# Scale factors of the head on GpSimd and ScalarE, zeroing inside the list, and mode switches known to the planner: a linear-attention and max-of-three feed-forward kernel

## The chip, the cores and the metric

The kernel runs on one core of a Trainium2 chip. The metric is the device time of one execution in microseconds (us). Engines are named as in the profile: PE is TensorE (PEld its weight loads), DVE is VectorE, ACT is ScalarE, POOL is GpSimd, SP is SyncE, whose queue issues most of the DMAs.

## The reference

Inputs r, k, v have the shape (4, 8, 768, 48) for batch, heads, sequence and head dimension; w and u are (8, 48). Each head keeps a 48x48 state:

```python
for t in range(S):
    kt, vt, rt = (k[:, :, t], v[:, :, t], r[:, :, t])
    cur = np.einsum('bhd,bhe->bhde', u[None] * kt, vt)
    y[:, :, t] = np.einsum('bhd,bhde->bhe', rt, state + cur)
    state = w[None, :, :, None] * state + np.einsum('bhd,bhe->bhde', kt, vt)
```

The result y, as 3072 tokens of 384 numbers, goes through a feed-forward layer with three up matrices (384x768) and one down matrix (768x384): `h = max(max(x @ w1, x @ w2), x @ w3)`, out = `h @ w_out`, all in float32.

## The kernel before

The recurrence is worked off in 12 chunks of 64 positions. A chunk has two parts q of 8 units each (a unit is a batch and a pair of heads on 2 x 64 partitions). In a chunk the decay w**t is multiplied into k and r (`scale`, L466), so that the state is only needed at the chunk's edges: `scores` are the products of keys and queries, `mask` keeps those of earlier positions, the diagonal holds r·(u k), `values` makes the output from masked scores and state, `keys` the addition to the state. Chunks 0 and 1 (`WHOLE`) do this in float32 on 64x64 quarters of PE (`whole`, L531), and take the diagonal from a product called the bonus (`bonus`, with `r_u` on ACT before it and `on_diagonal`, L558, on DVE behind it); their keys by position come from a product too (`flipped`, L565). Chunks 2 and 3 (up to `CORNERS`) split each operand into a high and a low float16 part and still use 64x64 quarters (L524). From chunk 4 on the split operands stand in `Block`s, tiles with two 64x64 blocks on the diagonal of a 128x128 square and zeros beside them; `spread` copies dense blocks into them by DMA, and PE uses its full array (L521). Up to chunk 2 DVE does the scalings; behind that GpSimd does (`helper`).

The feed-forward part works on a chunk's 256 tokens at a time: 18 `up` groups of 9 matmuls and 3 `down` groups of 18 (L651). x is also split in two float16 parts, and its last 96 rows are moved by six small DMAs (`x_last`, L635). The weights come as 64-bit words, eight tiles of 1152 KB; each is converted by ACT (`tops`, L340), DVE (`convert`, L344), ACT (`round_up`, L347) and DVE (`leave`, L350). Three buffers hold words (`raw64`); the tile `pw` of decay powers uses one of them at first. `stir` (L647) and `blank` (L640) are matmuls on a zero tile whose results nobody reads; there are 30 stirs of 3 matmuls, in a chain.

Ahead of the list, written by hand: loads of w, u and constants (L287 to L292), the zeroing of two tiles `ztop` and of the 14 blocks on POOL (L331, L415) and of the state (L439), and on DVE the decay powers (scans, L366) with the factors sc, wrt, wc, wcv, uw, dg, wck (L370 to L390).

Everything else is given to `Plan` by `do(due, engine, cost, fn, reads, writes, takes)`. Its `order` is a list scheduler that runs while the kernel is built: with a cost for each entry, a lag per engine, a model of the DMAs and of PE's clock, and start times for the engines (`free`), it picks the entry that can start first, and among those of one engine that can start within 0.02 us the one with the smallest due number. `SHIFT` adds a number per kind of entry and stage (five columns: due below 0, from 0, from 1, from 2, from 10) to the due number. The entries are then written out in order of their planned starts, and each engine takes its queue in that order; at run time an engine waits for semaphores, not for planned times.

Of the kernel before, what the change touches and what calls it, by code (L numbers as in the profile page):

```python
# [18 lines left out]
P = 128  # L19
# [52 lines left out]
class Plan:  # L72
# [4 lines left out]
    BEFORE, BEHIND, PHASE, LANES = 1.5, 1.0, 1.4, 8  # L77
    CLASSES = (0.0, 1.0, 2.0, 10.0)
    SHIFT = {
        "sp feat": (3.37, -2.28, 2.83, -0.27, 0),  # L80
        "sp tok": (-0.37, -1.28, 2.64, 0.03, 0),
        "dve tkf": (0, 0.35, 0, 0, 0),
        "pe turned": (0, -0.88, 0, 0, 0),
        "act tkt": (0, -2.47, 0, 0, 0),
        "dve kT": (-0.62, -26.75, 0, 0, 0),
        "dve rT": (1.01, -35.26, -13.5, 0, 0),
        "act ru": (1.08, 1.39, 0, 0, 0),
        "pe bo": (-1.74, -0.21, 0, 0, 0),
        "dve am": (0, -0.03, 0.19, 2.29, 8.79),
        "pe sc": (6.74, 6.37, 4.36, -0.11, 0.12),  # L90
        "pe va": (-1.39, -2.73, -1.75, -0.08, 0),
        "act xh": (1.82, -0.83, 0.07, -0.97, -3.12),
        "dve xl": (0.58, 0, -2.36, -1.28, 1.02),
        "sp x3": (-1.49, -1.21, 0.13, -4.67, -1.28),
        "act xsq": (0, 0.01, 0, 2.16, -1.69),
        "pe stir": (0, -4.85, -11.53, -2.89, 0),
        "sp word": (2.21, 2.24, 0, 0, 0),
        "act ztop": (4.76, 27.48, 0, 0, 0),
        "dve word": (0, -2.64, 0, 0, 0),
        "act his": (3.42, 1.73, 0, 0, 0),  # L100
# [144 lines left out]
def kernel(ctx, tc, feat, tok, wu, ut, ws, wo, cst, out):  # L245
# [594 lines left out]
    def act(columns):  # L843
        return 0.11 + 0.83e-3 * columns
# [304 lines left out]
```

## Time and profile before

| | us |
|---|---|
| median of three runs | 393.11 |
| the three runs | 390.78, 393.11, 394.2 |
| the profiled execution | 390.22 |
| its span, first to last instruction | 388.2 |
| PE busy / DVE busy / ACT busy / POOL busy | 375.1 / 243.0 / 244.3 / 185.2 |
| mean granted clock of PE | 0.993 |

The span is what the trace covers; 2.0 us of the execution lie around it. Busy shares are means over stages: in the head (to about 80 us) the recurrence's first chunks, the weights' conversion and the first feed-forward chunks overlap; the middle repeats chunk by chunk; the last 40 us are feed-forward alone.

### The profile page before, as it was taken

What the parts mean: (1) busy time and instruction counts of PE and PEld (TensorE: products, weight loads), DVE (VectorE), ACT (ScalarE), POOL (GpSimd) and SP (SyncE); (2) the same over time, 40 slices, a digit from 0 to 9 for tenths busy, and PEclk for the clock granted to TensorE, in tenths of its full rate; (3) what the DMA queues carried; (4) which work ended last, traced back from release to release, by engine and by line L of the source; (5) the groups of instructions that cost most, each with busy time, mean ns of one, the idle gap of its engine ahead of it and who ended that gap; (6) DMA issues with size and microseconds to landing.
All of it is one profiled execution on the core that took longest, in us unless ns stands there. A gap on an engine that the chain in (4) does not pass through costs nothing.

```text
span 388.2 us, 13560 instructions
## 1 busy us (share of the span) xinstructions
PE 375.1 (97%) x5652; PEld 337.8 (87%) x5652; DVE 243.0 (63%) x464; ACT 244.3 (63%) x618; POOL 185.2 (48%) x187
## 2 busy tenths in 40 slices
PE   6998999899999999999999999999999999999993
PEld 4877988788889999999999999999999999998883
DVE  7397999868568597558557557456467466232350
ACT  3478986587547566566566566566556865696621
POOL 9600032359975683673673683674673550020110
PEclk8999999999999999999999999999999999999999
DMA  8866673324852994994994996994994994903201
GB/s 273 342 206 248 207 281 116 138 82 143 231 186 88 298 251 125 288 299 134 276 300 156 279 234 163 300 284 128 305 256 114 279 253 104 293 24 144 77 2 49
DMA packets 27989, 77.23 MB, mean 199 GB/s; under 512 B 4881, under 2 KB 12561, under 8 KB 26897
## 3 DMA queue, kind: packets, MB, share of 16 engines
q1 hardware_dynamic: 27776, 76.19, 66.1%
q8 instruction: 46, 0.75, 0.9%
q14 instruction: 23, 0.18, 0.2%
q10 hardware_dynamic: 144, 0.10, 0.1%
HBM read 38.38 MB, written 4.72 MB: 111 GB/s over the span
## 4 chain that ended last, share of the span: by engine, by line
PE 91%; POOL 4%; DVE 1%; ACT 1%; issue 1%; DVEq 0%; POOLq 0%
PE psm L651 72%; PE psv L521 8%; PE psa L521 3%; PE psv L524 2%; PE psv L531 2%; PE psm L647 1%; PE psa L531 1%; PE psa L524 1%; PE psa L565 1%; POOL ztop L331 1%; ACT am L497 1%; POOL ktd L415 0%; POOL vd L415 0%; POOL kd L415 0%; POOL sb L415 0%
## 5 line engine op out<-in xcount | busy, mean ns | idle before, releaser
L651 PEld LDWEIGHTS <-w 128*128 128x128 f16 x2592 | 250.2, 98 | 29.6 <-issue 0.7
L651 PE MATMUL psm<-x,w 128*128 128x256 f16 x1944 | 219.7, 273 | 0.0
L679 POOL TENSOR_TENSOR hl<-m,hh 128x256 f16<-128x256 f32 x60 | 44.6, 745 | 130.2 <-ACT hh L673 125.1
L670 DVE SCALAR_TENSOR_TENSOR m<-psm,m 128x256 f32<-128x256 f32 x144 | 60.2, 419 | 60.6 <-PE psm L651 52.5
L673 ACT CAST hh<-m 128x256 f16<-128x256 f32 x72 | 29.0, 402 | 56.2 <-DVE m L670 55.8
L651 PE MATMUL psm<-hh,w 128*128 128x256 f16 x432 | 56.3, 273 | 0.5 <-issue 0.5
L466 POOL TENSOR_TENSOR feat<-feat,wrt 128x512 f32<-128x512 f32 x36 | 49.1, 1376 | 7.0 <-DMA feat<-in_feat_dram 7.0
L485 POOL TENSOR_TENSOR am<-tok,u_sb 128x384 f32<-128x384 f32 x18 | 20.8, 1157 | 45.1 <-DVE al L584 45.1
L449 ACT ACTIVATE junk<-tok 128x384 bf16<-128x384 f32 x72 | 37.4, 520 | 3.3 <-DMA tok<-in_tok_dram 2.1
L666 ACT ACTIVATE m<-psm 128x256 f32<-128x256 f32 x72 | 27.2, 378 | 14.0 <-PE psm L651 12.7
L651 PE MATMUL psm<-hl,w 128*128 128x256 f16 x216 | 33.4, 273 | 0.0
L628 DVE SCALAR_TENSOR_TENSOR x<-psv,x 112x512 f16<-112x512 f32 x24 | 16.5, 688 | 22.6 <-ACT x L624 22.1
L624 ACT ACTIVATE x<-psv 112x512 f16<-112x512 f32 x24 | 14.3, 594 | 15.4 <-PE psv L521 14.4
L521 PE MATMUL psv<-rh,sb 128*128 128x64 f16 x256 | 23.6, 193 | 0.0
L521 PE MATMUL psv<-ah,vb 128*128 128x64 f16 x256 | 23.6, 193 | 0.0
L521 PE MATMUL psv<-al,vb 128*128 128x64 f16 x128 | 22.7, 193 | 0.0
L521 PE MATMUL psv<-rl,sb 128*128 128x64 f16 x128 | 22.7, 193 | 0.0
L499 POOL TENSOR_TENSOR am<-cs,a 128x512 f32<-128x512 f32 x18 | 20.0, 1114 | 3.4 <-DVE a L490 3.3
L490 DVE TENSOR_REDUCE a<-am 128x8 f32<-128x384 f32 x20 | 11.0, 549 | 16.9 <-POOL am L486 16.9
L521 PEld LDWEIGHTS <-vb 128*128 128x128 f16 x384 | 21.1, 98 | 0.4
L574 DVE COPY_PREDICATED am<-cs,psa 128x512 f32<-128x512 int32 x24 | 17.7, 736 | 5.6 <-PE psa L521 5.0
L696 ACT ACTIVATE io<-psm 128x256 f32<-128x256 f32 x36 | 13.4, 381 | 11.1 <-PE psm L651 11.0
(119 smaller groups left out, 579.2 us busy)
## 6 DMA issues: line engine op xcount, KB each, us to landing
tok<-in_tok_dram SPq DMA_DIRECT2D x26, 576.0 KB, 6.3
feat<-in_feat_dram SPq DMA_DIRECT2D x24, 512.0 KB, 4.6
raw<-in_ws_dram SPq DMA_DIRECT2D x6, 1152.0 KB, 7.1
out_dram<-io SPq DMA_DIRECT2D x36, 128.0 KB, 4.8
vb<-vd SPq DMA_DIRECT2D x16, 256.0 KB, 6.9
sb<-sd SPq DMA_DIRECT2D x16, 256.0 KB, 6.9
kb<-kd SPq DMA_DIRECT2D x16, 256.0 KB, 6.6
vb<-vd SPq DMA_DIRECT2D x16, 248.0 KB, 6.8
```

Source lines behind the costliest of these rows:

```text
L449: nc.scalar.activation(out=junk[:, 0:U * D].rearrange("p (u d) -> p u d", u=U), in_=src, func=AF.Square, scale=scale, accum_out=stat[:, ki ...
L466: helper(c).tensor_tensor(out=t[n], in0=t[n], in1=tb, op=ALU.mult)
L485: helper(c).tensor_tensor(out=w.rearrange("p (g b) d -> p g b d", g=2), in0=t["r"], in1=by_token(u_sb, q), op=ALU.mult)
L499: helper(c).tensor_tensor(out=t["a"], in0=eye.unsqueeze(1).broadcast_to([P, U, C]), in1=t.pop("sum").unsqueeze(2).broadcast_to([P, U, C]), ...
L521: nc.tensor.matmul(out=ps[:, i, :], lhsT=block[k].on[a][i], rhs=prods[k](b, i), **flags)
L574: nc.vector.copy_predicated(out=t["a"], mask=strict.unsqueeze(1).broadcast_to([P, U, C]), data=t.pop("sc"))
L628: nc.vector.scalar_tensor_tensor(out=x_part(x, 1, q), in0=ps, scalar=sc_x(c), in1=x_part(x, 0, q), op0=ALU.mult, op1=ALU.subtract)
L651: nc.tensor.matmul(out=ps, lhsT=a, rhs=b, start=first and n == 0, stop=last and n == len(prods) - 1)
L666: nc.scalar.mul(out=m, in_=ps, mul=by)
L670: nc.vector.scalar_tensor_tensor(out=m, in0=ps, scalar=by, in1=m, op0=ALU.mult, op1=ALU.max)
L673: nc.scalar.copy(out=h[0][:, f, :], in_=m)
L679: lows_by(c, f).tensor_tensor(out=h[1][:, f, :], in0=m, in1=h[0][:, f, :], op=ALU.subtract)
```

## The change

Loads of w, constants and u are issued from ACT's queue, in this order, so that SP's starts with the features. wc, uw and dg are made on POOL, wcv and wck on ACT; sc stays on DVE as a scalar_tensor_tensor with a tile of ones. The scaling of u enters the list. tkf (decay factors for the token layout, transposed by PE into tkt) takes the buffer of `ru`. Blocks are no longer zeroed whole ahead of the list: entries "pad" zero only the columns that nothing writes, and the spreads read their keys. The state is not zeroed any more (chunk 0 writes it whole). `state1` is made on ACT. An entry says whether it uses quarters (`corner`), and a change between that and the full array costs `TURN` in the plan. Scores wait for the bonus, values of q = 1 for those of q = 0, the ups of a chunk for those of the chunk before (from chunk 2 on). `ah` and `al` get two buffers. `SHIFT` has new numbers in all its rows (a few are shown), and the engines' planned start times are new.

```diff
@@ -74,81 +74,83 @@
...
-    BEFORE, BEHIND, PHASE, LANES = 1.5, 1.0, 1.4, 8
+    BEFORE, BEHIND, PHASE, LANES, TURN = 1.5, 1.0, 1.4, 8, 0.095
...
     SHIFT = {
-        "sp feat": (3.37, -2.28, 2.83, -0.27, 0),
...
-        "dve tkf": (0, 0.35, 0, 0, 0),
...
-        "pe bo": (-1.74, -0.21, 0, 0, 0),
...
-        "pe sc": (6.74, 6.37, 4.36, -0.11, 0.12),
...
-        "pe stir": (0, -4.85, -11.53, -2.89, 0),
...
-        "act ztop": (4.76, 27.48, 0, 0, 0),
...
-        "pe kp": (5.05, -0.04, 0, 0, 0),
...
-        "pe up": (0, 23.33, 26.76, 0, 0.29),
...
+        "sp feat": (-1.56, 4.21, 2.31, 0.8, 0),
...
+        "act u": (0, 2.03, 0, 0, 0),
+        "pool pad": (0, -9.82, -1.24, 0, 0),
+        "dve tkf": (0, -2.54, 0, 0, 0),
...
+        "pe bo": (0.16, 2.71, 0, 0, 0),
...
+        "pe sc": (4.94, 1.67, -0.08, 0.08, 7.28),
...
+        "pe stir": (0, 0, -1.82, 7.69, -19.34),
...
+        "act ztop": (15.57, 7.02, 0, 0, 0),
...
+        "pe kp": (2.37, -0.61, 0, 0, 0),
...
+        "pe up": (0, 0, -0.08, 0.26, -1.61),
...
     }
...
@@ -216,6 +218,9 @@
...
+            if e == "pe" and p["corner"] != corner:
+                corner = p["corner"]
+                cost += self.TURN
@@ -284,12 +289,12 @@
...
     wu_sb = const.tile([P, 2, NP], F32, name="wu_sb")
-    nc.sync.dma_start(out=wu_sb, in_=wu)
+    nc.scalar.dma_start(out=wu_sb, in_=wu)
     w_sb, uf_sb = wu_sb[:, 0], wu_sb[:, 1]
+    cs = const.tile([P, 2 * P + 2], F32, name="cs")
+    nc.scalar.dma_start(out=cs, in_=cst)
     u_sb = const.tile([P, NP, D], F32, name="u_sb")
     nc.scalar.dma_start(out=u_sb, in_=ut)
-    cs = const.tile([P, 2 * P + 2], F32, name="cs")
-    nc.sync.dma_start(out=cs, in_=cst)
@@ -366,64 +371,68 @@
         nc.vector.tensor_tensor_scan(
...
+    one4 = ones[:, 0:NP]
     sc = const.tile([P, NP], F32, name="sc")
     nc.vector.reciprocal(out=sc, in_=pw[:, :, C // 2])
-    nc.vector.tensor_scalar(out=sc, in0=sc, scalar1=SC_R, scalar2=None, op0=ALU.mult)
+    nc.vector.scalar_tensor_tensor(out=sc, in0=sc, scalar=SC_R, in1=one4, op0=ALU.mult, op1=ALU.mult)
     wrt = const.tile([P, NP, C], F32, name="wrt")
     nc.vector.tensor_tensor(out=wrt, in0=pw[:, :, 0:C], in1=sc.unsqueeze(2).broadcast_to([P, NP, C]), op=ALU.mult)
     wkt = wrt[:, :, ::-1]
-    wc = const.tile([P, NP], F32, name="wc")
-    nc.vector.tensor_copy(out=wc, in_=pw[:, :, C])
-    wcv = const.tile([P, NP], F32, name="wcv")
-    nc.vector.tensor_scalar(out=wcv, in0=wc, scalar1=SC_V, scalar2=None, op0=ALU.mult)
-    uw = const.tile([P, NP], F32, name="uw")
-    nc.vector.tensor_tensor(out=uw, in0=uf_sb, in1=w_sb, op=ALU.mult)
+    wc, wcv, wck, uw = (const.tile([P, NP], F32, name=n) for n in ("wc", "wcv", "wck", "uw"))
+    nc.gpsimd.tensor_tensor(out=wc, in0=pw[:, :, C], in1=one4, op=ALU.mult)
+    nc.gpsimd.tensor_tensor(out=uw, in0=uf_sb, in1=w_sb, op=ALU.mult)
     dg = const.tile([P, NP, D], F32, name="dg")
-    nc.vector.tensor_tensor(out=dg, in0=eye[:, 0:D].unsqueeze(1).broadcast_to([P, NP, D]), in1=wc.unsqueeze(2).broadcast_to([P, NP, D]), op=ALU.mult)
-    tkf = const.tile([P, NP, 2, C], F32, name="tkf")
+    nc.gpsimd.tensor_tensor(out=dg, in0=eye[:, 0:D].unsqueeze(1).broadcast_to([P, NP, D]), in1=wc.unsqueeze(2).broadcast_to([P, NP, D]), op=ALU.mult)
+    nc.scalar.mul(out=wcv, in_=wc, mul=SC_V)
+    nc.scalar.mul(out=wck, in_=wc, mul=SC_KT / SC_R)
...
     def both():
+        tkf = work.tile([P, U, C], F32, name="ru").rearrange("p (g h) s -> p g h s", h=2)
+        turned.append(tkf)
         for hh in range(2):
             nc.vector.tensor_tensor(out=tkf[:, :, hh, :], in0=wkt, in1=wck.unsqueeze(2).broadcast_to([P, NP, C]), op=ALU.mult)
...
-    wck = const.tile([P, NP], F32, name="wck")
-    nc.vector.tensor_scalar(out=wck, in0=wc, scalar1=SC_KT / SC_R, scalar2=None, op0=ALU.mult)
     tkt = const.tile([P, NP, D], F32, name="tkt")
-    nc.scalar.mul(out=u_sb, in_=u_sb, mul=SC_A)
...
+    def u_scaled():
+        nc.scalar.mul(out=u_sb, in_=u_sb, mul=SC_A)
...
     turned = []
...
     def turn():
         tps = psa.tile([P, NP, P], F32, name="psa")
         for g in range(NP):
-            nc.tensor.transpose(out=tps[:, g, :], in_=tkf[:, g].rearrange("p a s -> p (a s)"), identity=ident)
+            nc.tensor.transpose(out=tps[:, g, :], in_=turned[0][:, g].rearrange("p a s -> p (a s)"), identity=ident)
         turned.append(tps)
...
     def turned_back():
         for hh in range(2):
             hs = slice(hh * C, (hh + 1) * C)
-            nc.scalar.copy(out=tkt[hs], in_=turned[0][hs, :, hh * C:hh * C + D])
...
+            nc.scalar.copy(out=tkt[hs], in_=turned[1][hs, :, hh * C:hh * C + D])
...
+    W = P if CORNERS < NCH else C
...
     class Block:
...
-        def __init__(self, name, w):
-            n = 2 * U * w
-            t = bd.tile([P, n + P - w], F16, name=name)
-            nc.gpsimd.memset(t.bitcast(F32), 0.0)
-            self.flat, self.w = t[:, 0:n], w
+        def __init__(self, name, used=None):
+            n, w = 2 * U * W, used or 0
+            t = bd.tile([P, n + P - W], F16, name=name)
+            self.flat = t[:, 0:n]
             self.dense = self.flat.rearrange("p (s u n) -> p s u n", s=2, u=U)
-            self.on = [[t[:, (s * U + i) * w:(s * U + i) * w + P] for i in range(U)] for s in range(2)]
+            self.on = [[t[:, (s * U + i) * W:(s * U + i) * W + P] for i in range(U)] for s in range(2)] if W == P else None
+            self.blank = self.dense.bitcast(F32)[:, :, :, w // 2:]
...
-    kd, ktd, vd, sd = ([Block(f"{n}{q}", P) for q in range(2)] for n in ("kd", "ktd", "vd", "sd"))
-    kb, ktb = (Block(n, P) for n in ("kb", "ktb"))
-    vb, sb = ([Block(f"{n}{q}", P) for q in range(2)] for n in ("vb", "sb"))
+    kd, ktd, vd, sd = ([Block(f"{n}{q}", w) for q in range(2)] for n, w in (("kd", C), ("ktd", D), ("vd", D), ("sd", D)))
+    kb, ktb = (Block(n) if W == P else None for n in ("kb", "ktb"))
+    vb, sb = ([Block(f"{n}{q}") if W == P else None for q in range(2)] for n in ("vb", "sb"))
@@ -436,7 +445,6 @@
...
     state = const.tile([P, NP, B, D], F32, name="state")
-    nc.gpsimd.memset(state, 0.0)
@@ -880,7 +888,7 @@
...
     def spreading(c, due, dst, src, keys, name):
         if c >= CORNERS:
-            dma(due, lambda: spread(nc.sync, dst, src), 2.4, reads=keys, writes=[name], n=2)
+            dma(due, lambda: spread(nc.sync, dst, src), 2.4, reads=[*keys, *(("pad", n) for n in range(14))], writes=[name], n=2)
@@ -907,7 +915,7 @@
...
-        do(due - 0.16, h, 2 * cost, lambda: product(c, q), reads=[t], takes=[("am", ("am", c, q))], writes=[("kdec", c, q)], near=0.55)
+        do(due - 0.16, h, 2 * cost, lambda: product(c, q), reads=[t, "u"], takes=[("am", ("am", c, q))], writes=[("kdec", c, q)], near=0.55)
@@ -936,17 +944,17 @@
...
-        do(due - 0.27, "pe", 0.96, lambda: bonus(c, q), reads=[f, ("kT", c, q), ("ru", c, q)], takes=[("psa", ("bo", c, q))], counts=0.5)
+        do(due - 0.27, "pe", 0.88, lambda: bonus(c, q), reads=[f, ("kT", c, q), ("ru", c, q)], writes=[("bonus", c, q)], takes=[("psa", ("bo", c, q))], counts=0.5, corner=True)
...
-        scored(c, q, due, [f, ("kT", c, q), ("rT", c, q)])
+        scored(c, q, due, [f, ("kT", c, q), ("rT", c, q), ("bonus", c, q)])
...
     def whole_values(c, q, due):
         sbs = [("sd", q), ("rT", c, q), ("feat", c, q)] if c else []
-        do(due, "pe", 0.92 * (1 + (c > 0)), lambda: values(c, q), reads=[("am", c, q), ("tok", c, q), *sbs], takes=[("psv", ("va", c, q))], counts=0.5)
+        do(due, "pe", 0.89 * (1 + (c > 0)), lambda: values(c, q), reads=[("am", c, q), ("tok", c, q), *sbs, *[("valued", c)] * q], writes=[("valued", c)] * (not q), takes=[("psv", ("va", c, q))], counts=0.5, corner=True)
...
@@ -963,14 +971,14 @@
...
         if c + 1 < WHOLE:
-            do(due + 0.06, "dve", 0.5, lambda: nc.vector.tensor_scalar(out=state1[q], in0=sf, scalar1=S16, scalar2=None, op0=ALU.mult), reads=[s], writes=[("sd", q)])
+            do(due + 0.06, "act", act(U * D), lambda: nc.scalar.mul(out=state1[q], in_=sf, mul=S16), reads=[s], writes=[("sd", q)])
...
     def valued(c, q, due, reads):
         reads = [*reads, *held(c, [("sdh", q), ("sdl", q)], ("sb", q))]
@@ -1012,7 +1020,8 @@
...
-                do(due + 0.035 * i, "pe", 0.983, mul, reads=[*x, *((a, f, h) for a in ("his", "lo") for h in parts[i])], takes=[("psm", ("up", c, f, i))])
+                do(due + 0.035 * i, "pe", 0.983, mul, reads=[*x, *((a, f, h) for a in ("his", "lo") for h in parts[i]), *[("upped", c - 1)] * (c > 1)],
+                   writes=[("upped", c)] * (f == NF - 1), takes=[("psm", ("up", c, f, i))])
@@ -1051,7 +1060,11 @@
...
-    do(0.1, "dve", 0.7, both, writes=["tkf"])
+    do(0.1, "act", 0.36, u_scaled, writes=["u"])
+    if W == P:
+        for n, b in enumerate([*kd, *ktd, *vd, *sd, kb, ktb, *vb, *sb]):
+            do(0.5 + 0.1 * n, "pool", 1.0 if n > 7 else 0.7, lambda b=b: nc.gpsimd.memset(b.blank, 0.0), writes=[("pad", n)])
+    do(0.1, "dve", 0.7, both, takes=[("ru", "tkf")])
@@ -1080,7 +1093,7 @@
...
-    order = plan.order(dict(pe=1.5, dve=5.2, act=3.0, pool=13.0, sp=1.6))
+    order = plan.order(dict(pe=1.5, dve=4.7, act=4.4, pool=5.4, sp=0.75))
...
```

## Rows read from the trace of the kernel before

**Rows 1.** The page of the profile: span, and PE's busy time, share and instructions.

```profile
span 388.2 us, 13560 instructions
PE 375.1 (97%) x5652; PEld 337.8 (87%) x5652; DVE 243.0 (63%) x464; ACT 244.3 (63%) x618; POOL 185.2 (48%) x187
```

**Rows 2.** Busy time by stretch: stretch and its length, busy us (instructions) of PE, PEld, DVE, ACT and POOL, granted clock of PE, DMA share, GB/s. The last two rows are of DVE alone.

```profile
8.00:9.00 1.00, 1.00 (x7) 0.69 (x6) 1.00 (x3) 0.81 (x3) 1.00 (x2) 0.50 1.04 436
...
40.00:50.00 10.00, 10.00 (x185) 9.02 (x181) 9.90 (x15) 9.11 (x14) 0.91 (x2) 1.00 0.71 247
...
70.00:80.00 10.00, 8.52 (x281) 7.24 (x279) 8.22 (x17) 7.94 (x23) 2.00 (x2) 1.00 0.40 141
...
140.00:170.00 30.00, 30.00 (x420) 27.43 (x419) 22.20 (x39) 17.63 (x48) 17.12 (x18) 1.00 0.84 234
...
0.00:40.00 40.00, 27.56 (x51) 0.96 0.72 259
40.00:70.00 30.00, 29.86 (x44) 1.00 0.55 196
```

**Rows 3.** Groups of PE's instructions by line and shape: count, busy us, mean ns of one, idle before.

```profile
L651 PE MATMUL psm<-x,w 128*128 128x256 f16 x1944 | 219.7, 273 | 0.0
...
L647 PE MATMUL psm<-still 128*128 128x256 f16 x90 | 13.6, 306 | 1.1 <-DVE still L266 1.1
```

**Rows 4.** The chain of waits that ended last, in order of time: start, us, what. The stretch in which it leaves PE.

```profile
63.49 5.03 PE psm L651 x45
...
69.16 1.21 DVE tok L505
...
71.20 2.03 ACT am L497 x8
...
74.47 0.73 PE psv L524 x44
```

**Rows 5.** Timeline of DVE in the head: start us, us, line, operation, out<-in; in brackets the idle time before and what ended it.

```profile
3.65 0.18 DVE L370 RECIPROCAL sc<-raw 128x4 f32<-128x4 f32 x1
3.86 0.74 DVE L371 TENSOR_SCALAR sc<-sc 128x4 f32<-128x4 f32 x1
...
4.64 0.42 DVE L373 TENSOR_TENSOR wrt<-raw,sc 128x256 f32<-128x256 f32 x1
4.98 0.54 DVE L376 COPY wc<-raw 128x4 f32<-128x4 f32 x1
...
6.36 0.08 DVE L443 MEMSET stat<- 128x24 f32 x1
6.48 0.76 DVE L387 TENSOR_TENSOR tkf<-wrt,wck 128x256 f32<-128x256 f32 x2
7.16 2.49 DVE L466 TENSOR_TENSOR feat<-feat,wrt 128x512 f32<-128x512 f32 x4
...
14.10 0.69 DVE L558 TENSOR_TENSOR am<-psa,cs 128x512 f32<-128x512 f32 x1 [4.45 <-PE psa L531]
...
16.68 0.36 DVE L966 TENSOR_SCALAR state<-state 128x384 f32<-128x384 f32 x1 [1.11 <-ACT state L600]
```

**Rows 6.** Timeline of POOL, ACT and PE in the head, in the same form.

```profile
7.30 0.81 PE L398 MATMUL psa<-cs,tkf 128*128 128x128 f32 x4 [2.11 <-DVE tkf L387]
...
8.81 0.91 ACT L548 ACTIVATE ru<-feat,uw 128x256 f32<-128x256 f32 x2
...
12.90 1.15 PE L531 MATMUL psa<-ru,feat 64*64 64x64 f32 x32
...
15.26 0.74 POOL L439 MEMSET state<- 128x768 f32 x1
...
16.03 0.54 ACT L600 COPY state<-psv 128x192 f32<-128x192 f32 x2 [0.97 <-POOL state L439]
...
17.12 1.48 ACT L340 CAST ztop<-raw 128x1152 f16<-128x1152 bf16 x1
...
36.82 2.14 PE L651 MATMUL psm<-x,w 128*128 128x256 f16 x18
```

**Rows 7.** SP's queue: the issue of the first features (timeline), and all loads of features (page: count, KB each, median us from issue to landing).

```profile
1.66 0.43 SPq L272 DMA_DIRECT2D feat<-in_feat_dram  x1
...
feat<-in_feat_dram SPq DMA_DIRECT2D x24, 512.0 KB, 4.6
```

**Rows 8.** Groups by line and shape that are nearest to the moved products: a GpSimd product of 256 columns over the whole run (page), and of the first 47 us ScalarE's groups and GpSimd's smallest memset.

```profile
L679 POOL TENSOR_TENSOR hl<-m,hh 128x256 f16<-128x256 f32 x60 | 44.6, 745 | 130.2 <-ACT hh L673 125.1
...
L429 ACT ACTIVATE sd<-state 128x384 f16<-128x384 f32 x2 | 1.0, 522 | 0.0
...
L449 ACT ACTIVATION_READ_ACCUMULATOR junk<-state 128x1 f32 x4 | 0.8, 192 | 0.0
...
L1136 POOL MEMSET const-float32-1.0<- 128x1 f32 x1 | 0.1, 98 | 0.0
```

**Rows 9.** Timeline of POOL and DVE: a GpSimd product, and the same scaling on DVE beside it and alone.

```profile
53.76 1.44 POOL L679 TENSOR_TENSOR hl<-m,hh 128x256 f16<-128x256 f32 x1 [2.69 <-ACT hh L673]
...
54.92 0.83 DVE L466 TENSOR_TENSOR feat<-feat,wrt 128x512 f32<-128x512 f32 x1
...
56.34 0.68 DVE L466 TENSOR_TENSOR feat<-feat,wrt 128x512 f32<-128x512 f32 x1
```

**Rows 10.** Timeline of PE's weight loads at the change from the full array to quarters, with the idle time before it.

```profile
62.54 0.83 PEld L524 LDWEIGHTS <-kd 64*64 64x64 f16 x48 [0.21 <-issue]
```

More of the change, by code (lines that the diff above doesn't have):

```diff
@@ L146 @@
+        "pe count": (0, 0, 0, 0, -0.24),
+        "dve flag": (0, 0, 0, 0, 0.89),
     }
@@ L149, in __init__, with do @@
         self.bufs, self.todo, self.wrote, self.read = bufs, [], {}, {}
-    def do(self, due, eng, cost, fn, reads=(), writes=(), takes=(), move=0, near=0, parts=1, counts=1.0):
+    def do(self, due, eng, cost, fn, reads=(), writes=(), takes=(), move=0, near=0, parts=1, counts=1.0, corner=False):
         n = len(self.todo)
@@ L168, in do @@
         need.discard(n)
-        self.todo.append(dict(n=n, due=due, eng=eng, cost=cost, fn=fn, need=need, takes=takes, move=move, near=near, parts=parts, counts=counts, kind=kind, stage=stage, base=base, touch={*reads, *writes, *new}))
+        self.todo.append(dict(n=n, due=due, eng=eng, cost=cost, fn=fn, need=need, takes=takes, move=move, near=near, parts=parts, counts=counts, corner=corner, kind=kind, stage=stage, base=base, touch={*reads, *writes, *new}))
     def order(self, free):
@@ L185, in order @@
         ready = [p["n"] for p in self.todo if not p["need"]]
-        out, taken = [], {pool: [] for pool in self.bufs}
+        out, taken, corner = [], {pool: [] for pool in self.bufs}, False
         def earliest(p):
@@ L577, in a_high @@
         t = raws[c, q]
-        t["ah"] = work.tile([P, U, C], F16, name="ah")
+        t["ah"] = work.tile([P, U, C], F16, name="ah", bufs=2)
         nc.scalar.copy(out=t["ah"], in_=t["a"])
@@ L918, in before_keys @@
         if c < WHOLE:
-            do(due - 0.30, "pe", 0.76, lambda: flipped(c, q), reads=[("feat", c, q), ("kT", c, q)], takes=[("psa", ("kp", c, q))], counts=0.5)
+            do(due - 0.30, "pe", 0.70, lambda: flipped(c, q), reads=[("feat", c, q), ("kT", c, q)], takes=[("psa", ("kp", c, q))], counts=0.5, corner=True)
             do(due - 0.30, "act", act(U * D), lambda: flipped_back(c, q), reads=[("kp", c, q)], takes=[("kt", ("kt", c, q))])
@@ L956, in keyed @@
     def keyed(c, q, due, reads):
-        do(due, "pe", 0.76 if c < WHOLE else 0.64 if c < CORNERS else 0.62, lambda: keys(c, q), reads=reads, takes=[("psv", ("ke", c, q))], counts=0.5 if c < WHOLE else 1.0)
+        do(due, "pe", 0.72 if c < WHOLE else 0.64 if c < CORNERS else 0.62, lambda: keys(c, q), reads=reads, takes=[("psv", ("ke", c, q))], counts=0.5 if c < WHOLE else 1.0, corner=c < CORNERS)
         s = ("state", q)
@@ L972, in valued @@
         reads = [*reads, *held(c, [("sdh", q), ("sdl", q)], ("sb", q))]
-        do(due, "pe", 1.43 if c < CORNERS else 1.42, lambda: values(c, q), reads=[*reads, ("ah", c, q), ("al", c, q), ("rh", c, q), ("rl", c, q)], takes=[("psv", ("va", c, q))])
+        do(due, "pe", 1.43 if c < CORNERS else 1.42, lambda: values(c, q), reads=[*reads, ("ah", c, q), ("al", c, q), ("rh", c, q), ("rl", c, q), *[("valued", c)] * q], writes=[("valued", c)] * (not q), takes=[("psv", ("va", c, q))], corner=c < CORNERS)
         leave_x(c, q, due)
```

120 lines of the change are left out of this document (59 added, 61 removed).

## The prediction

> **What bounds the kernel now.** First the page: TensorE (PE) is busy for 375.1 of 388.2 us [rows 1], so the end can only come forward by the time in which PE idles or does work that counts for nothing. Then the stretches [rows 2]: from 140 to 170 us, as in all the middle, PE is busy for the whole 30 us, and nothing in the change takes matmuls from there. The gaps are in the first 80 us. Then PE's groups [rows 3]: 90 matmuls on a zeroed tile ("stir", 13.6 us) fill waits in that head. The first matmul of the feed-forward part starts at 36.82 us [rows 6], and from there PE is nearly full until 68.5 us.
>
> There the chain of waits is the important view [rows 4]: it leaves PE and runs through VectorE's decay of the tokens and ScalarE's eight diagonals before PE can go on at 74.47. VectorE was busy 29.86 of the 30 us before 70, and PE only 8.52 of the 10 us after 70 [rows 2]. So PE has used up what VectorE had prepared. Where VectorE idled is before 40 us: 27.56 us busy of 40 [rows 2]. **A head that is shorter on PE alone would wait again near 70 us; a gain has to be an earlier VectorE.** That is my measure for each part.
>
> **The scale factors.** VectorE's order by hand is: scans, reciprocal 0.18, sc 0.74 (at 3.86), wrt (at 4.64), and from 4.98 the copy wc, then wcv, uw, dg and wck, until the memset of stat at 6.36 and the first listed work, tkf, at 6.48 [rows 5]. The change takes wc to wck away: 6.36 - 4.98 = 1.4 us. The op on sc stays, in another form; from 3.86 to 4.64 it held the queue 0.78 us, while the reciprocal on the same 128x4 tile took 0.18. Between these ends (nothing won, 0.6 won) I take 0.5, as the neighbour is of the same size and on the same engine. Listed work starts 1.9 us earlier, at about 4.6.
>
> Is the rest there by then? tkf needs wck, now scan, GpSimd, ScalarE. No GpSimd product of four columns is shown: from below a 0.10 us memset, from above the 0.745 of 256 columns; for ScalarE 0.19 (one column read out [rows 8]) and 0.27 (half of the two copies of 192 columns at 16.03 [rows 6]). From the scans' end at 3.6, wck is then ready between 4.1 and 5.0 counting both ScalarE products, at the worst 0.4 us behind a start at 4.6 and still 1.4 us ahead of 6.48. dg and uw follow on GpSimd by 5.8 at the worst, ahead of their readers. Feature loads move to the front of SP's queue: the first was issued at 1.66 behind two others [rows 7] and now goes at about 0.75; with the 4.6 us that such a load takes to land [rows 7] that is 5.4, just when a tkf of 0.76 that starts at 4.6 is through. The three small loads now pass one after another through ScalarE's queue, which has nothing else until wcv; u is third and has no early reader. I cost that at nothing; if the cover fails, the factors wait about 0.8 us (two issues of 0.4).
>
> **The zeroing.** GpSimd's list of memsets ended with state at 15.26 to 16.0, and ScalarE's first copy into state waited for it, 0.97 us [rows 6]. Left as it was, this would have kept a chunk 0 that comes 1.9 us earlier from gaining anything behind that copy: the memsets do not depend on VectorE. Its removal is therefore the condition of the first term and has no term of its own. The smaller memsets go behind the factors on GpSimd; their first readers are the spreads of chunk 4, far behind 80 us, and GpSimd has little else so early (0.91 us busy from 40 to 50 [rows 2]). Cost nothing; without that cover, one memset, of about the 0.74 that state took, would stand in front of a product.
>
> **state1 to ScalarE.** Two products of 0.36 [rows 5] leave VectorE and become two of about 0.5 on ScalarE (0.522 for the same columns, [rows 8]). VectorE gains 0.7, but ScalarE was busy 9.11 of the 10 us from 40 to 50 [rows 2] and feeds the weights. Between 0 and 0.7 I take 0.4.
>
> **The order.** VectorE idled from 9.65 to 14.10 for the bonus scores [rows 5]. Their left operand was ready at 9.72 (ScalarE, 8.81 + 0.91), but PE did two other products first and started the bonus at 12.90 [rows 6]: up to 3.2 us too late. Behind PE's idle 2.11 us the clock had fallen to its 1.2 GHz level (granted 0.50 from 8 to 9 [rows 2, 6]). In the new list the scores wait for the bonus by a key, and the flips are due behind it; I take half, 1.6, between 0 (ordered as late as before) and 3.2. That VectorE would use the time is likely: weight 0 could be converted, which waited until 17.12 [rows 6].
>
> **Corners.** Some 15 groups of 64-row products lie among 128-row ones before 122 us; each enters with 0.21 us in which the weight loads stand still [rows 10], of which little shows in PE's own row. If a few of these turns go, it is between 0 and 15 x 0.21 = 3.2; I take 0.3, since the list must still alternate.
>
> **Sum.** 1.9 + 0.4 + 1.6 + 0.3 = 4.2 us. Against the profiled execution, 390.22 (span 388.2 and 2.0 around it), this gives 386.0. That execution was faster than all three runs shown (390.78, 393.11, 394.2); the mean of the four is 392.1, so 1.9 more has to be added for a typical run: **388 us** (387.9).
>
> **The rivals.** *The gain is absorbed* (0 to 3 us; 389.1 to 392.1). VectorE and GpSimd can hold each other up: beside GpSimd's product of 53.76 a scaling took 0.83 us, alone 0.68 [rows 9], and beside memsets the copy of four columns took 0.54 and the tensor_scalar 0.74 [rows 5]. Now three GpSimd products run beside sc, wrt and tkf. If VectorE waits out each, at up to 0.745, that is 2.2 us: 4.2 - 2.2 leaves 2.0, so 390.1. For it speak the rows; against it, that the two small products are over before 5 us. The Trainium skill (SBUF — State Buffer, "Who interferes with whom") says that a VectorE op with two SBUF inputs contends with a GpSimd op that reads SBUF, and not with one that only writes it. By that rule the new neighbours are worse for wrt and tkf than the memsets were; the 0.83 agrees with it. The same band holds the case that the last weights come no earlier because their words land no earlier.
>
> *The whole head moves* (6.5 to 9 us; 383.1 to 385.6): all of the 3.2, all of the switches that lie in the head, and VectorE's idle 4.45 us filled with weight 0. For it: VectorE idles 12.4 us before 40. Against it: the weights' words, which land no faster.
>
> *The stirs stand in the way* (slower). In the new table the stirs from the tenth on have due numbers from -9.3, ahead of most products. Freed early, 20 of them at 3 x 0.113 = 0.34 us (1944 matmuls of the same size in 219.7 us [rows 3]) put 6.8 us between the bonus and the values of chunk 0, and PE takes its queue in order. Against the 2.6 us of the other terms that is 4.2 slower: 396.3. It decides from 2.6 us of stirs that are not in a wait, eight of them. Against it: PE idled up to the transposes at 7.30, and the more stirs go there, the fewer are left.
>
> That the change does not do what it says has no case of its own here: the ops are moved in plain sight; only the order that the list works out is not seen, and this is in the bands.
>
> **How the numbers follow.** Forecast (gain 3 to 6.5, 385.6 to 389.1) 0.47; absorbed 0.30; whole head 0.13; stirs 0.10. A measurement of this kernel tells 1% from no change, that is below 389.2 or above 397.0 against 393.11. Faster: 0.44 of the forecast and 0.13 make 0.57. Slower: half of the stirs' case, 0.05. Same 0.38. The range runs from 383 to 393: it takes in the forecast, the absorbed case with 1 us of scatter above it and about half of the early one, some 0.81. The forecast's own range is 385.6 to 389.1.
>
> **What would show it.** tkf or the first scaling of features near 4.6 instead of 6.48; no wait of ScalarE for GpSimd at its first state copy; the bonus of chunk 0 ahead of the flips, with on-diagonal work before 11 us; the first feed-forward matmul at 33 us or earlier; VectorE less idle before 40. Wrong it is if these come early and PE idles more than 1.5 us between 60 and 80, if stirs stand between the bonus and the values, or if sc, wrt and tkf are longer than 0.3, 0.42 and 0.76.

## The result and the profile after

The changed kernel takes 394.15 us (median of 20 runs, 392.49 to 396.93), the kernel before 392.83 in the same session (20 runs): a ratio of 1.0052, 95% interval 1.0028 to 1.0076. Forecast were 388.0 us and a range up to 393. Five of the 20 runs of before took 402.7 to 408.1 us; ratios, here and below, compare the other runs alone. The profiled execution took 393.33 us, 3.1 more than the one of before (390.22); by the ratio it is 2.0.

The page of the profile after, its span and busy times, which answer to [rows 1]:

```profile
span 391.6 us, 13595 instructions
PE 377.9 (97%) x5652; PEld 338.8 (87%) x5652; DVE 244.1 (62%) x457; ACT 241.8 (62%) x622; POOL 178.3 (46%) x189
```

PE has the same 5652 instructions and is busy 2.8 us longer, the stirs' share of it 0.7 us (14.3 us against 13.6). So the page alone doesn't say where the 3 us came from. The head does not look bad. The timeline of DVE in it, which answers to [rows 5]:

```profile
4.67 0.84 DVE L371 TENSOR_TENSOR_SCAN raw<-wu_sb,ones 128x64 f32<-128x64 f32 x4 [3.57 <-DMA wu_sb<-in_wu_dram]
5.54 0.18 DVE L376 RECIPROCAL sc<-raw 128x4 f32<-128x4 f32 x1
5.75 0.20 DVE L377 SCALAR_TENSOR_TENSOR sc<-sc,ones 128x4 f32<-128x4 f32 x1
5.98 0.69 DVE L379 TENSOR_TENSOR wrt<-raw,sc 128x256 f32<-128x256 f32 x1
6.63 0.08 DVE L451 MEMSET stat<- 128x24 f32 x1
6.78 0.76 DVE L393 TENSOR_TENSOR ru<-wrt,wck 128x256 f32<-128x256 f32 x2
7.46 2.49 DVE L474 TENSOR_TENSOR feat<-feat,wrt 128x512 f32<-128x512 f32 x4
14.32 0.69 DVE L566 TENSOR_TENSOR am<-psa,cs 128x512 f32<-128x512 f32 x1 [4.37 <-PE psa L539]
```

The five operations are gone and sc takes 0.20 in place of 0.74, but the scans begin 1.9 us later than before (2.77): the 4 KB of W|U, now issued on ScalarE's queue at 0.75, beside the features on SP's, land after 3.82 us. So the list starts at 6.78, not 4.6 (before 6.48). wrt takes 0.69 in place of 0.42.

Busy time by stretch after, with the columns of [rows 2]:

```profile
0.00:40.00 40.00, 36.24 (x705) 30.77 (x707) 26.38 (x45) 26.70 (x48) 12.79 (x23) 1.00 0.69 259
40.00:80.00 40.00, 39.51 (x653) 34.97 (x649) 34.94 (x58) 30.35 (x71) 11.38 (x11) 1.00 0.53 185
80.00:115.00 35.00, 33.29 (x683) 28.41 (x682) 30.98 (x47) 22.39 (x64) 32.29 (x28) 1.00 0.56 160
115.00:170.00 55.00, 54.09 (x798) 49.15 (x791) 34.88 (x65) 31.93 (x85) 27.89 (x30) 1.00 0.79 220
170.00:380.00 210.00, 210.00 (x2798) 191.43 (x2796) 116.09 (x244) 128.95 (x354) 93.98 (x100) 1.00 0.71 197
```

Before, PE was busy 34.26, 38.52, 35.00, 55.00 and 210.00 us in these. The change closed gaps before 80 us and opened others between 80 and 170, where there had been none, and where DVE was busy 24.48 of 35 us and is now busy 30.98.

Busy time counts stirs and stretched waits as work, so I also counted PE's useful matmuls begun by a given time, each once, at the rate at which a run of its kind passes (0.109 us a feed-forward matmul, 0.029 one of the recurrence on the full array, 0.030 and 0.016 those in float32 and float16 on quarters). Each column is one profiled execution; a difference of some tenths between two columns can be scatter (e11 has after's list up to 79 us and differs from it by 0.6 at 80). The kernels e1 to e13 are told of below.

| us of work begun by | before | after | e1 | e5 | e7 | e9 | e11 | e13 |
|---|---|---|---|---|---|---|---|---|
| 36 us | 15.7 | 18.3 | 16.7 | 18.3 | 15.6 | 18.2 | 18.5 | 20.2 |
| 80 us | 57.2 | 58.7 | 58.2 | 60.1 | 57.2 | 58.4 | 59.3 | 61.6 |
| 115 us | 91.5 | 90.3 | 92.6 | 94.5 | 88.9 | 91.2 | 91.8 | 94.1 |
| 170 us | 146.7 | 144.3 | 147.7 | 149.5 | 142.7 | 144.6 | 147.0 | 149.3 |
| 380 us | 357.2 | 354.6 | 358.3 | 358.6 | 353.0 | 354.2 | 357.0 | 359.2 |

After was 2.6 us ahead at 36 and 1.5 at 80, 1.2 behind at 115 and 2.4 at 170, and kept that to the end. **So the head was won and the middle lost**, and the experiments have to say by which part of the change.

### The profile page after: what moved, and what is told of

It is laid out like the page before. It is cut to its first block, busy times and chain, and to the rows that moved or that the text cites. A ratio compares the mean times of both kernels' runs of the same rounds, so it can differ in the third digit from the quotient of the medians.

```text
span 391.6 us, 13595 instructions
## 1 busy us (share of the span) xinstructions
PE 377.9 (97%) x5652; PEld 338.8 (87%) x5652; DVE 244.1 (62%) x457; ACT 241.8 (62%) x622; POOL 178.3 (46%) x189
## 4 chain that ended last, share of the span: by engine, by line
PE 72%; DVE 8%; DMA 7%; issue 4%; POOL 4%; ACT 3%; SPq 0%; DVEq 0%; ACTq 0%; POOLq 0%
PE psm L659 54%; PE psv L529 7%; PE psa L529 3%; DMA kb<-kd 2%; PE psa L539 2%; PE psm L655 2%; DMA raw<-in_wo_dram 2%; DMA tok<-in_tok_dram 2%; DVE m L678 1%; POOL feat L474 1%; PE psv L539 1%; POOL hl L687 1%; PE psa L573 1%; DMA wu_sb<-in_wu_dram 1%; DVE w L355 1%
## 5 line engine op out<-in xcount | busy, mean ns | idle before, releaser
L659 PE MATMUL psm<-x,w 128*128 128x256 f16 x1944 | 223.2, 273 | 0.5 <-DVE m L678 0.5
L687 POOL TENSOR_TENSOR hl<-m,hh 128x256 f16<-128x256 f32 x60 | 43.8, 735 | 149.9 <-ACT hh L681 136.6
L474 POOL TENSOR_TENSOR feat<-feat,wrt 128x512 f32<-128x512 f32 x36 | 47.3, 1326 | 11.1 <-DMA feat<-in_feat_dram 11.1
L507 POOL TENSOR_TENSOR am<-cs,a 128x512 f32<-128x512 f32 x18 | 21.0, 1168 | 3.9 <-DVE a L498 3.8
L529 PEld LDWEIGHTS <-sb 128*128 128x128 f16 x384 | 20.0, 98 | 0.0
L494 POOL TENSOR_TENSOR am<-am,tok 128x384 f32<-128x384 f32 x18 | 19.1, 1062 | 1.4
```

Source lines behind the costliest of these rows:

```text
L474: helper(c).tensor_tensor(out=t[n], in0=t[n], in1=tb, op=ALU.mult)
L494: helper(c).tensor_tensor(out=w, in0=w, in1=units(t["k"]), op=ALU.mult)
L507: helper(c).tensor_tensor(out=t["a"], in0=eye.unsqueeze(1).broadcast_to([P, U, C]), in1=t.pop("sum").unsqueeze(2).broadcast_to([P, U, C]), ...
L529: nc.tensor.matmul(out=ps[:, i, :], lhsT=block[k].on[a][i], rhs=prods[k](b, i), **flags)
L659: nc.tensor.matmul(out=ps, lhsT=a, rhs=b, start=first and n == 0, stop=last and n == len(prods) - 1)
L687: lows_by(c, f).tensor_tensor(out=h[1][:, f, :], in0=m, in1=h[0][:, f, :], op=ALU.subtract)
```

## The experiments

Ratios are to the kernel before, with 95% intervals.

**The operations without the order, and the order without the operations.** e1 is the changed kernel in the old list's order, e2 the old operations in the new one (with tkf in the buffer of `ru` and two buffers each for `ah` and `al`, which that order needs). The cut is e1's; e2's is of the same form.

```diff
-    order = plan.order(dict(pe=1.5, dve=4.7, act=4.4, pool=5.4, sp=0.75))
+    order = [plan.todo[int(n)] for n in FROZEN.split()]
```

> The changed kernel's operations, loads and buffers, written out in the order that the list of before had (zeroing first on GpSimd, the scaling of u ahead of the copies into tkt). Theory ORDER (the new list is what costs: it lags from 85 us on): no loss against before, 0 to 2 us faster, and PE idle for less than 1.5 us between 80 and 170. Theory LATE LOAD (w, u land 1.9 us later beside the features, and the list, planned for less, breaks behind it): as slow as the changed kernel or slower, about +2 us against before, since the load is as late here.

> The operations and loads of before (factors on VectorE, whole zeroing ahead of the list, state1 on VectorE; the buffers of ah, al and ru as in the changed kernel) in the order of the changed kernel's list. ORDER: about 2 us slower than before, with the same lag behind 85 us as the changed kernel. LATE LOAD: equal to before within 1 us or faster, since w lands at 2.8 us here.

e1: 390.34 us, 0.9938 (0.9904 to 0.9972). e2: 395.84 us, 1.0057 (1.0024 to 1.0089). The new operations gain 0.6% in the old order. The new order loses with either set of operations, and in it the new operations gain nothing (1.0052 against 1.0057). From e1 to the changed kernel it is 1.0052 - 0.9938, 1.1% or 4.5 us (1.6 either way by the two intervals). Theory ORDER had 0 to 2 us of gain for e1 and about 2 us of loss for e2, and e1's PE is full from 80 to 170: this came, with a little more of each.

**The late load.** e3 is the changed kernel with W|U first on SP's queue, e4 the kernel before with the new loads' places, e5 is e1 with W|U first.

```diff
-    nc.scalar.dma_start(out=wu_sb, in_=wu)
+    nc.sync.dma_start(out=wu_sb, in_=wu)
```

> The changed kernel with one edit: the load of w and u factors is issued first on SP's queue, ahead of the features, as before; the list is the same to the last entry. LATE LOAD: scans start at 2.8 instead of 4.67 us, listed VectorE work near 4.9, and the time falls by 2 to 3 us, to that of before or below. ORDER: the head is earlier by up to 1.9 us, but less than 1 us of it reaches the end.

> The kernel before with one edit: w, constants and u are issued from ScalarE's queue and the features go first on SP's, as in the changed kernel. LATE LOAD: scans start near 4.7 us and the end comes about 1.9 us later. ORDER: the scans are late too, but the end moves by less than 1 us, because chunk 0 waits behind GpSimd's memsets until 16 us and VectorE idles from 9.65 to 14.10 anyway.

> The changed kernel's operations in the order of before, and the load of w issued first on SP's queue. If the head's 1.9 us on VectorE are worth what the prediction gave them, 1 to 2.5 us faster than the same without the early load (0.9938 of before): 0.988 to 0.992 of before. If VectorE waits for PE at 9.65 to 14 us anyway, no difference from 0.9938.

e3: 394.05 us, 1.0014 (0.9976 to 1.0052); e4: 394.36, 1.0015 (0.9974 to 1.0056); e5: **388.75, 0.9917 (0.9886 to 0.9948)**, the best of all and better than both kernels. e3 gives back 1.5 us, between its two theories. e4's scans are as late as after's (4.68), and the end moves by 0.6 us (interval -1.0 to 2.2), nearer to theory ORDER, but 1.9 is not shut out. e5 lies within what the early load was to give. Timeline of DVE in e3:

```profile
2.98 0.84 DVE L371 TENSOR_TENSOR_SCAN raw<-wu_sb,ones 128x64 f32<-128x64 f32 x4 [1.87 <-DMA wu_sb<-in_wu_dram]
4.29 0.70 DVE L379 TENSOR_TENSOR wrt<-raw,sc 128x256 f32<-128x256 f32 x1
5.09 0.76 DVE L393 TENSOR_TENSOR ru<-wrt,wck 128x256 f32<-128x256 f32 x2
```

The new place of the load is the cause of the late scans: 2.98 in place of 4.67, and the list starts at 5.09, 1.4 us earlier than before. e3 changes two things at once, the queue of W|U and, since it goes ahead of the features, their issue from 0.75 to 1.20. That ScalarE's queue is not slow by itself is seen in e3 too: the constants, 129 KB issued on it at 0.75, landed after 2.3 us. What is missing of the 1.9 is 0.2 of the scans (2.98 against 2.77) and 0.3 of wrt, 0.70 in place of 0.42; GpSimd's new products uw and dg run beside it, but they were not taken away by themselves. At the end the 1.7 us are worth 0.2 to 0.4% (e5 against e1, e3 against after), 0.8 to 1.5 us, with overlapping intervals.

**Which part of the list.** e6 takes the new order up to 68 us and then the old, e7 the reverse.

> The changed kernel with every entry that its list plans before 68 us (about 75 us on the chip) in the new order and all others in the order of before. If the loss lies in the new list behind that point (its lag grows from 85 to 170 us): 0.990 to 0.996 of before. If the new head leaves other engines behind, so that any tail would lag: 1.003 or more.

> The other half: the order of before up to 68 us of its plan, and the rest in the new order. If the loss lies behind that point: 2 to 4 us slower than the changed operations in the old order (0.9938), so 0.999 to 1.005 of before, with VectorE busier than 28 us between 80 and 115. If it lies in the head: within 0.992 to 0.996.

e6: 392.29 us, 0.9988 (0.9964 to 1.0012), between its two expectations. e7: 397.82, 1.0128 (1.0096 to 1.0161), worse than either of its own. The new tail loses 80 to 115 us as in after (PE 32.97 of 35 busy, in e6 34.13) and again up to 170 (54.03 of 55, in e6 55.00). e6 still lies 0.5% above e1. A list that is cut and joined also loses at the joint (PE busy 37.52 us from 40 to 80 in e6, in before 38.52), so these two tell the place, not the size.

**The zeroing, alone.** e8 is the kernel before without the memset of the state by GpSimd.

```diff
-    nc.gpsimd.memset(state, 0.0)
```

> The kernel before without the zeroing of the state on GpSimd, nothing else. The prediction held this wait (0.97 us of ScalarE) to be what kept an earlier VectorE from helping: 0 to 1 us faster (0.9975 to 1.0). If the 0.62% of the changed operations in the old order comes from it alone: 0.994.

390.48 us, 0.9955 (0.9933 to 0.9977): one line gives 1.8 us, more than the 0 to 1 expected and less than the whole gain of e1 (0.994). ScalarE's first copy into the state moves from 16.03 to 14.95, with no idle time before it. The traces show less than the ratio: the first feed-forward matmul comes at 36.48 (before 36.82), and the work begun by 380 us is 0.7 ahead. Where the other 1.1 us come from stays open; the interval is 0.9 us either way.

**GpSimd beside VectorE.** In after GpSimd is busy 32.29 of the 35 us from 80, and VectorE's operations there have grown. e9 replaces GpSimd's products of chunks 3 to 5 by a product of one column and two memsets of the same tile; these chunks' products are left out, and the final check of the range.

```diff
-        helper(c).tensor_tensor(out=t[n], in0=t[n], in1=tb, op=ALU.mult)
+        helped(c, t[n], t[n], tb)   # c in 3..5: one column, then two nc.gpsimd.memset(out, 0.01)
```

> The changed kernel, its list unchanged, with GpSimd's products of chunks 3 to 5 (scalings, u k r, decay, diagonals) replaced by a product of one column per unit and two memsets of the whole tile: GpSimd is busy about as long, but hardly reads SBUF. The products of these chunks are left out, so the output is not the reference's, and the closing range check is switched off. Theory PORT (in the new order VectorE's two-input operations fall beside GpSimd's products and wait for each other): between 80 and 115 us the low parts of state, values and queries fall from 1.37, 1.22 and 1.16 us to about 0.55, 0.55 and 0.69, PE idles for less than 0.7 us there instead of 1.7, and the time falls by 1.5 to 3 us. Theory LATE PRODUCTS (PE waits because the new order asks for chunk 3 sooner than the chain through GpSimd can give it): the idle time stays above 1.2 us and less than 1 us is won.

393.58 us, 1.0024 (0.9988 to 1.006), 0.3% below after, with overlapping intervals. VectorE's groups by line and shape, 80 to 115 us, in after (count, busy, mean ns, idle before):

```profile
L445 DVE SCALAR_TENSOR_TENSOR sd<-state,sd 128x384 f16<-128x384 f32 x3 | 4.1, 1371 | 0.0
L445 DVE SCALAR_TENSOR_TENSOR vd<-tok,vd 128x384 f16<-128x384 f32 x3 | 3.7, 1223 | 0.0
L498 DVE TENSOR_REDUCE a<-am 128x8 f32<-128x384 f32 x3 | 1.6, 545 | 1.6 <-POOL am L494 1.6
```

and in e9:

```profile
L506 DVE TENSOR_REDUCE a<-am 128x8 f32<-128x384 f32 x3 | 1.7, 553 | 4.6 <-POOL am L477 4.6
L445 DVE SCALAR_TENSOR_TENSOR sd<-state,sd 128x384 f16<-128x384 f32 x3 | 1.6, 548 | 0.0
L445 DVE SCALAR_TENSOR_TENSOR vd<-tok,vd 128x384 f16<-128x384 f32 x3 | 1.6, 547 | 0.0
```

These two operations, with two operands in SBUF, take 2.5 and 2.2 times as long beside GpSimd's products (the others with two such operands 1.5 to 3 times); the reduction, with one, takes the same. With GpSimd nearly only writing, the two are at 548. The Trainium skill (SBUF — State Buffer, "Who interferes with whom") says that a VectorE instruction with two SBUF inputs contends with a GpSimd one that reads SBUF, and not with one that only writes it; here the trace agrees with it (1371 ns beside the products, 548 beside the memsets).

In the old order GpSimd is busy 30.25 us in this stretch, and there is contention too (vd 817 in the mean), but part of the wait falls on the other engine. Timeline of DVE and POOL in before:

```profile
97.61 0.54 DVE L436 SCALAR_TENSOR_TENSOR vd<-tok,vd 128x384 f16<-128x384 f32 x1
98.08 0.55 DVE L436 SCALAR_TENSOR_TENSOR sd<-state,sd 128x384 f16<-128x384 f32 x1
96.18 3.35 POOL L499 TENSOR_TENSOR am<-cs,a 128x512 f32<-128x512 f32 x2
```

Here vd and sd keep their 0.54 and 0.55, and the second of GpSimd's two products takes 2.03 us, where 1.04 is the median of its kind. So what the new order changes is, at least in part, which of the two waits.

Of the two theories neither came whole: the durations fell as PORT had it, but PE still idles 1.11 us from 80 to 115 (1.71 in after), and about 1 us is won in place of 1.5 to 3. The work begun by 115 us rises by 0.9 (91.2 against 90.3), but by 170 only 0.3 of that is left and by 380 nothing, so something later takes it back.

**The planner's constant.** e10 sets the cost that the planner puts on a mode switch to zero and keeps the table of due times.

> The changed kernel with TURN = 0 in the planner, that is, the same operations and the same table of shifts, planned anew without the price of a mode switch. If the table carries (its numbers suit the work and not one list only): within 1% of the changed kernel, and without the switches' price some more of them. If the table fits only the list it was made for: more than 3% slower, with PE idle in many places behind the head.

437.07 us, 1.1138 (1.1007 to 1.127); PE waits 8.5 us at once for a spread block and 7.1 for ScalarE. This table of shifts did not carry to a list with another `TURN` (two executions), and the run tells nothing of the switches themselves. From before to after pauses at them grew: PE's weight loads stand still at entries into quarter mode (L532), with no wait that the profile names, 13 times for 3.9 us in after, and 7 times for 1.5 in before (L524).

**ScalarE's queue.** From 115 to 170 us PE has one wait in after, at 159. ScalarE's timeline of after shows where it comes from:

```profile
157.75 0.52 ACT L457 ACTIVATE junk<-tok 128x384 bf16<-128x384 f32 x1 [2.96 <-DMA tok<-in_tok_dram]
158.18 0.19 ACT L457 ACTIVATION_READ_ACCUMULATOR junk<-tok 128x1 f32 x1
158.40 0.52 ACT L457 ACTIVATE junk<-tok 128x384 bf16<-128x384 f32 x1
158.83 0.18 ACT L457 ACTIVATION_READ_ACCUMULATOR junk<-tok 128x1 f32 x1
158.92 0.39 ACT L681 CAST hh<-m 128x256 f16<-128x256 f32 x1
```

and PE's:

```profile
159.36 0.38 PE L659 MATMUL psm<-hh,w 128*128 128x256 f16 x2 [0.83 <-ACT hh L681]
```

ScalarE, which works in order, stands 2.96 us at a square sum that nobody needs before the end of the run, because its tokens have not landed. Two square sums later comes the cast hh, for which PE waits. The page's row of these sums in after:

```profile
L457 ACT ACTIVATE junk<-tok 128x384 bf16<-128x384 f32 x72 | 37.5, 520 | 16.5 <-DMA tok<-in_tok_dram 15.5
```

Before, that last number was 2.1, in e7 14.6, in e2 14.2. e11 puts the 34 sums of r and v from chunk 3 on 4 us later in the new list and moves nothing else; e12 adds e9's edit.

```diff
-FROZEN = '''... (the new list)'''
+FROZEN = '''... (the new list, "act sq" of r and v at start + 4.0)'''
```

> The changed kernel with its own list, but the 34 square sums that ScalarE takes of freshly loaded r and v blocks (chunk 3 on) stand 4 us later in it; nothing else moves. Theory A: part of what the new list loses from 80 us on is ScalarE waiting in its own order at a square sum for the load (16.5 us of idle at that line, 15.5 of it ended by the load, against 3.3 before), with the down projections' casts queued behind it: then that idle time falls below 6 us, the stall of TensorE at 158 to 159 us goes, and the time is 0.8 to 1.5 us below the changed kernel's 394.1, at 392.6 to 393.3. Theory B: the waiting only takes up slack of ScalarE: the idle time moves to other lines and the time stays at 393.6 to 394.6. Theory C: the squares then stand ahead of other casts that are late, and the time rises by over 1 us.

> The kernel with the square sums 4 us later, and in addition GpSimd's products of chunks 3 to 5 are replaced by a one-column product and two memsets of the same tile (their results are left out, and the range check with them). Theory A: GpSimd's products beside VectorE's two-input operations and ScalarE's waits at the square sums make up most of the loss between 80 and 170 us: together they give back 2 to 3 us, 391 to 392. Theory B: what sets the end is the order itself (which stage runs when), so that VectorE and ScalarE in time again gain under 1 us: 393.2 to 394.

e11: 391.92 us, 0.9990 (0.9963 to 1.0017). e12: 390.70, 0.9956 (0.9926 to 0.9987). What ended ScalarE's idle time at the sums in e11, and e11's stretches:

```profile
  DVE state L610: 3.1, 4
  DMA tok<-in_tok_dram: 0.2, 1
```

```profile
80.00:115.00 35.00, 33.79 (x751) 29.16 (x749) 31.11 (x47) 22.04 (x62) 33.10 (x28) 1.00 0.60 168
115.00:170.00 55.00, 55.00 (x738) 50.09 (x736) 35.10 (x67) 32.87 (x90) 29.01 (x31) 1.00 0.80 229
```

From 115 to 170 PE is full again, and the work begun by 380 us is 357.0, nearly that of before (357.2). The other engines' and SP's instructions stand in the same order as in after. The gain, 0.6% or 2.4 us (1.4 either way), is larger than the 0.8 to 1.5 expected. PE's idle time from 80 to 170 gives 1.4 of it (2.62 us in after, 1.21 in e11); the rest is within the interval and not explained. VectorE stays at 31.11, so the contention is left, and e12 takes it away: 0.3% more, with intervals that overlap. (e12's profiled execution, 394.26, was the longest of its 13, with a wait of 1.9 us for the DMA of x, so its rows are not used.) The idle time alone need not be a loss: e4 has 9.1 us of it and is as fast as before within its interval. In e5, which has 12.0, the work goes on at e1's rate from 80 to 170 (89.4 us against 89.5); behind that it falls 1.5 back, in one wait of 1.5 us for a spread block, and whether the sums have a part in that is not shown. In after it counts where a cast stands behind it on which PE waits.

**What was left open by then.** e13 is e11 with W|U first; e14 is e8 with state1 on ScalarE, in the old order.

```diff
-nc.vector.tensor_scalar(out=state1[q], in0=sf, scalar1=S16, scalar2=None, op0=ALU.mult)
+nc.scalar.mul(out=state1[q], in_=sf, mul=S16)
```

> The changed kernel with the square sums 4 us later in its list and, in addition, W|U loaded first on SP's queue. Theory A: the list's start at about 5 us instead of 6.8 now reaches the end, since the waits that swallowed it behind 115 us are gone: 1 to 1.7 us below e11, ratio 0.995 to 0.997 to the kernel before, 390.3 to 391. Theory B: another in-order wait between 60 and 115 us takes it: ratio 0.998 to 1.000, within 0.5 us of e11.

> The kernel before without the zeroing of the state by GpSimd, and with the scaled state of chunk 0 written by ScalarE in place of VectorE, in the old list's order. Theory A: the term of 0.4 us taken for that step is real, VectorE bounds the head and all its work there counts: 0.3 to 0.5 us below the kernel with the memset alone removed (ratio 0.9955), so 0.994 to 0.995. Theory B: it is hidden or falls on a loaded ScalarE: 0.9955 or more.

e13: 390.41 us, 0.9963 (0.9935 to 0.9992). e14: 390.27, 0.9959 (0.992 to 0.9997). The earlier load reaches the end with about 1 us (work begun 2.3 us ahead of e11 at 80 and at 170), as theory A had it, intervals overlapping. state1 alone gives nothing that shows beside e8's 0.9955, as theory B had it; its 0.4 us is smaller than the interval, 1.5 us either way. e13 stays above e5, with intervals that overlap a little: in the old order the new operations did best.

## Why the prediction was wrong

**The scale factors** (1.9 taken). The five operations and sc went as told, sc to 0.20 (the 0.5 was right). The step that failed is "I cost that at nothing". The three small loads went through ScalarE's queue; I priced their issue (0.8 at worst) and not W|U's landing beside 512 KB loads, though DVE's start hangs on it: 1.9 us, all that the term had for the start of the list, of which 0.8 to 1.5 reach the end. The second miss is wrt, 0.3 longer beside dg (GpSimd, from 5.89 for 0.51); I had named this contention as a rival, and set against it only that the two small products are over before 5 us.

**The zeroing** (a condition without a term). It was the largest gain of the parts that were run alone, 1.8 us by e8 (0.9 to 2.6). I argued that the memset would hold up a chunk 0 that comes earlier. But it held up the old one already: ScalarE's idle 0.97 [rows 6] was itself a gain to be had. The ratio says that it lay on the path; of the way to the end the traces show only 0.7 us.

**state1** (0.4): nothing in e14, but a term of this size can't be told from nothing there.

**The order** (+1.6 taken, between 0 and 3.2) is the step that failed and decided. I gave it bounds without a loss, since I looked for its effect only in the head; measured, the new order costs 4.5 us, and with e1's gain of 2.4 that makes the changed kernel's 2.0 us of loss. In the head the 1.6 did not even come: the flips (L573) stay ahead of the bonus (L539). PE's timeline of after:

```profile
9.28 1.95 PE L573 MATMUL psa<-dg,feat 64*64 64x48 f32 x32
11.16 1.46 PE L655 MATMUL psm<-still 128*128 128x256 f16 x6
12.55 1.71 PE L539 MATMUL psa<-ru,feat 64*64 64x64 f32 x32
```

The bonus begins at 12.55 (before 12.90) though its operand was ready at 10.3 (ScalarE, 9.41 + 0.91), and the on-diagonal product at 14.32 (14.10). Of the 2.2 us between, the end of the flips takes 0.8 and the six stir matmuls 1.4. The flips could begin at 9.28, before that operand was there; the planner takes first what can start first, and a due number decides only within 0.02 us, so that flips due behind the bonus need not stand behind it. A list that is planned anew is new everywhere. From e1 to after 4.5 us are lost by the ratios, 3.9 by the work begun between 80 and 170 (89.5 against 85.6). Of the 4.5, 2.4 come back when ScalarE's square sums stand later (e11; 1.4 of it is seen as idle time of PE) and 1.3 when GpSimd's products are taken away too (e12 against e11, less sure). Some 0.7 us remain, within the intervals.

**Corners** (0.3): there were more pauses at switches, not fewer; what they cost was not tried.

**The rivals.** *Absorbed* had the contention right, but in the wrong place: by the head rather than by the middle. *The whole head moves* did not come: the first feed-forward matmul is 2.6 us earlier, not 6.5. *Stirs*: the longest block of them, 36 matmuls from 22.55 to 26.65, lies behind chunk 0's values and was there before (39 from 22.33); six matmuls stand in front of the bonus and six between it and the values. But the work begun by 36 us is 2.6 ahead, so they did not decide. No rival held a loss behind 80 us; I had set that aside with "PE is busy for the whole 30 us" [rows 2], which is a statement on the old list.

Of the signs: the copy without its wait came, and the first feed-forward matmul at 34.18 (36.82 before, 33 asked). The start near 4.6, the bonus ahead of the flips, on-diagonal work before 11 us and a VectorE less idle before 40 (13.6 us, before 12.4) did not.

**Right for the wrong terms:** scale factors and state1 summed to 2.3, and e1, which holds them in the old order, gained 2.4. That is luck: e1 has the late load, which takes away the first, and a zeroing that gave 1.8 and had no term. e5, with the load first, gained 3.3.

Not settled: how the 0.7 us and e6's 0.5% divide between the new head and the joints of a cut list. e9 and e12 leave products out and so change what follows them in time; the contention was not tried in another way. The new zeroing of the blocks and the scaling of u in the list were not run by themselves.

## What to carry to other kernels

When a change re-plans a list, price the order as a part of its own, with a loss among its bounds, and test it by running the new operations in the old order. On an engine that works in order, an instruction with no reader must not stand right behind the load that it reads; look at who queues behind it. A load on which the first instruction hangs is priced from issue to landing, in the company in which it will be.

## What had not been expected of the hardware

A 4 KB load issued at 0.75 us on ScalarE's queue, together with one of 512 KB on SP's, landed after 3.82 us. In e3, where the first feature load is issued at 1.20, both loads issued at 0.75 landed early: the 4 KB on SP's queue after 2.1 us, and 129 KB on ScalarE's after 2.3. Whether the large load is issued at the same time or 0.45 us later so goes with 1.7 us for a small one.

Where a VectorE operation and a GpSimd product meet, either can bear the wait: sd took 1371 ns in the mean in after, from 80 to 115 us; in before one sd took 545 and GpSimd's product beside it 2.03 us in place of 1.04.
